# Both heads' exponentials in one instruction over two PSUM banks, in the first four head pairs of an attention and mixer kernel

## The chip, the cores and the metric

One core of one Trainium2 chip. The metric is device time in microseconds (us), from three runs; next to it stands one profiled execution, whose trace gives every number on a single instruction. PE is TensorE's matmuls, PEld its weight loads, DVE is VectorE, ACT ScalarE, POOL GpSimd, SP SyncE.

## The reference

Eight batches, eight heads, 576 tokens, head size 64, 16 extra "beacon" keys and values ahead of the tokens. Attention is causal over the tokens; a low-rank mix along the sequence (rank 32) with a residual follows, then a two-layer MLP (512 to 2048 to 512) with another residual.

```python
k_all = np.concatenate([beacon_k, k], axis=2)          # 592 keys
v_all = np.concatenate([beacon_v, v], axis=2)
scores = scale * np.matmul(q, k_all.transpose(0, 1, 3, 2))
scores = np.where(causal, -1000000000.0, scores)
a = softmax(scores)
x = np.matmul(a, v_all)                                # to (batch, 576, 512)
u = x + (x.transpose(0, 2, 1) @ U @ V).transpose(0, 2, 1)
out = u + np.maximum(u @ w_ch1, 0.0) @ w_ch2
```

## The kernel before, in words

The work goes by pairs of heads: 32 pairs, four to a batch; pairs 0 to 3 are the first batch. For a pair, blocks of transposes on PE (lines 275 and 281) turn q and k, DVE copies them to SBUF as `qT` and `kT` (line 308; the beacons apart, line 313), and `score_units` computes the transposed scores, keys on partitions. The keys of one head fall into four groups of columns (496, 464, 496 and 208 wide, numbered 0 to 3), each in a PSUM bank of its own. One visit takes two groups of both heads: `sc[0]` groups 0 and 1, `sc[1]` groups 2 and 3. The two heads' score matmuls (line 348) stand on two halves of the array and run side by side. ACT then takes the exponential of each group and head, one instruction each (line 354), from its bank into `expt`, a buffer of one head; four such buffers serve two pairs in turn. A head's attn*V (`av_unit`, line 397) is 15 small matmuls into one bank, a reciprocal and a product on DVE (405, 406).

The causal mask is laid in one of two ways. For the pairs in `ON_PE` (0, 1, 4) PE adds a large negative number to the bank before the scores (line 340). For the others DVE takes a minimum with a mask over the exponentials afterwards (`mask_head`, lines 324 and 326).

The order of all engines is written out by hand (`manual_schedule`): an engine runs its instructions in the order in which they are emitted, and the waits between engines are put in by the build from what each instruction reads and writes. PSUM's eight banks are handed out by `pst`, a queue of emptied banks; each result is a tile of its own, in the bank that has been empty longest. `emptying` gives a bank back when its last reader is emitted. `keep_warm` and `idle` (line 250) emit matmuls without use.

After the first batch's four pairs `first_mix` computes the mix in three pieces: `head` (the matmuls `qtp`, line 489), `begin` (413), `rest` (506). Between them stand the first parts (`part`) of the MLP's first layer (`gps`, line 534), whose results ACT (547) and DVE (549) evict with a relu into `gT`. From there on `fill(n)` puts MLP units between the steps of attention: tiles of 512 tokens, 16 units of the first layer, then 16 of the second (`cps`, line 560). The first `fill(3)` of the stage is followed by the transposes of pair 4. The last 128 rows of the last tile go by `c_piece` in three column pieces (256, 128 and 128 wide, `cph`, line 589), each with its addition (594) and its store (596).

Loads are issued by POOL in the order of emission: q, k and v of the first batches, w1 in four pieces and w2 in two (`emit_w2`, line 195).

Of the kernel before, what the change touches and what calls it, by code (L numbers as in the profile page):

```python
# [1 line left out]

# [28 lines left out]
def kernel(  # L31
# [123 lines left out]
    uT = const.tile([P, NCC, B * S], F16, name="uT", tag="uT")  # L155
    rec = const.tile([P, B * H, NT, 1], F32, name="rec", tag="rec")
    NE = 4
    expts = [const.tile([P, EW], F16, name=f"expt{i}", tag=f"expt{i}") for i in range(NE)]
    kTs = [const.tile([P, NH2, NC * P], F16, name=f"kT{i}", tag=f"kT{i}") for i in range(2)]
    vss = [const.tile([P, NC * H * E], F16, name=f"vs{i}", tag=f"vs{i}") for i in range(2)]  # L160

# [26 lines left out]
        fs = ds(FF // 4 * i, FF // 4)  # L188
        nc.gpsimd.dma_start(out=w1[:, :, fs], in_=w1r[:, :, fs])

    def emit_w2():
        w2r = moe_w_ch2.rearrange("(dc p) c -> p dc c", p=P)
        for i in range(2):
            dcs = ds(NDC // 2 * i, NDC // 2)
            nc.gpsimd.dma_start(out=w2[:, dcs, :], in_=w2r[:, dcs, :])

# [118 lines left out]

        return [lambda: one(1, qT, 0), lambda: one(0, kT, Nb)]

    def score_units(c, qT, kT, ex, early=False):  # L320

        def mask_head(i):
            e4 = ex[i][:, 0:EW].rearrange("p (g w) -> p g w", w=SLOT)[:, :, 0:P]
            nc.vector.tensor_tensor(out=e4, in0=e4, in1=bigmask, op=ALU.min)  # L324
            o, n = blk[(4, 4)], nq[4]
            nc.vector.tensor_tensor(
                out=ex[i][0:n, ds(o, n)], in0=ex[i][0:n, ds(o, n)], in1=mask[0:n, 0:n], op=ALU.min
            )

        def visit(gs, idle=0, by_head=True, between=None):  # L330
            turn = [(g, i) for i in range(2) for g in gs] if by_head else [(g, i) for g in gs for i in range(2)]
            ps = {(g, i): pst([P, 512], F32, name=f"sps{i}") for g, i in turn}
            keep_warm(ps[gs[0], 0], idle)
            if early:
                for g in gs:
                    for i in range(2):
                        for ch, qa, w, o in groups[g]:
                            if ch in (g, 4):
                                n = nq[ch]
                                nc.tensor.matmul(  # L340
                                    ps[g, i][:, ds(o, n)], identb, negmask[:, min(ch, 1), 0:n],
                                    start=ch == g, stop=False, skip_group_check=True,
                                )
            for g in gs:
                for ch, qa, w, o in groups[g]:
                    for i in range(2):
                        hp = slice(D * i, D * i + D)
                        nc.tensor.matmul(  # L348
                            ps[g, i][:, ds(o, w)], kT[hp, c, ds(P * ch, P)], qT[hp, c, ds(qa, w)],
                            start=not early, stop=True, skip_group_check=early,  # L350
                        )

            def exps(g, i):
                nc.scalar.activation(  # L354
                    out=ex[i][:, ds(SLOT * g, gw[g])], in_=ps[g, i][:, 0 : gw[g]], func=AF.Exp, scale=scale
                )
# [15 lines left out]

# [145 lines left out]
    def mlp_units(t0, n, dst, flip, turned=True, last=False):  # L518
# [59 lines left out]
                emptying(ps)  # L578
                nc.sync.dma_start(out=dst(i, m), in_=ob[:m, :])

        def c_piece(i, part):

            o, w, d0, d1 = [
                (0, 2 * P, 0, NDC // 2), (0, 2 * P, NDC // 2, NDC), (2 * P, P, 0, NDC), (3 * P, P, 0, NDC)
            ][part]
            if d0 == 0:
                cps["t"] = pst([P, w], F32, name="cph")
            for dc in range(d0, d1):
                nc.tensor.matmul(  # L589
                    cps["t"], gT["t"][:, dc, ts(i, P)], w2[:, dc, ds(o, w)], start=(dc == 0), stop=(dc == NDC - 1)  # L590
                )
            if d1 == NDC:
                ob = outp.tile([P, w], F32, name="oh", tag="ob")
                nc.vector.tensor_tensor(out=ob, in0=cps["t"], in1=gT["u"][:, i, ds(o, w)], op=ALU.add)
                emptying(cps["t"])
                nc.sync.dma_start(out=dst(i, P)[:, ds(o, w)], in_=ob)

        units += [lambda dc=dc: g_unit(dc) for dc in range(NDC)]
        for i in range((n + P - 1) // P):
            c = c_piece if last and i == n // P - 1 else c_unit  # L600
            units += [lambda i=i, part=part, c=c: c(i, part) for part in range(4)]
        return units, g_part

# [105 lines left out]
    def qkT_of(p):  # L709
# [6 lines left out]
                turns[i] = in_pair(prs[p])[i]  # L716
        return qkT_units(turns, qTs[b], kTs[b % 2], c, copies, Ls[0][0][0] if p == 0 else None)

    def expts_of(p):
        return [expts[(2 * p + i) % NE] for i in range(2)]  # L720

    def scores_of(p):
        b, c = divmod(p, NH2)
        return score_units(c, qTs[b], kTs[b % 2], expts_of(p), p in ON_PE)

    def masks_of(p):
        scores_of(p)[2]()
# [1 line left out]
    def av_of(p):  # L729
        b, c = divmod(p, NH2)  # L730
        if c == 0:
            xbs[b] = xbp.tile([P, NT, DM], F16, name="xb", tag="xb")
        return [
            lambda i=i: av_unit(b, 2 * c + i, expts[(2 * p + i) % NE], vss[b % 2], xbs[b]) for i in range(2)
        ]


    NF = 2
    ON_PE = (0, 1, 4)
    AHEAD = 16  # L740

    DT0 = 4
# [50 lines left out]
    with tc.manual_schedule(engines={ENG.PE, ENG.Activation, ENG.DVE, ENG.SP, ENG.Pool}):  # L793
# [58 lines left out]
        mask_head = sc[3]  # L852
# [298 lines left out]
```

## Time and profile before

| | |
|---|---|
| median of three runs | 351.49 us (350.92 to 352.44) |
| the profiled execution's own time | 351.05 us |
| its span, first to last instruction | 349.4 us |
| mean granted TensorE clock | 0.998 |
| PE busy | 342.7 us, 98% |
| ACT busy | 164.2 us, 47% |
| DVE busy | 190.2 us, 54% |

The span is cut by the profile into stretches and groups. A row of the timeline has the start in the span, the time from there to the end of the last instruction merged into it, the engine, the line, the operation, what is written and read, and a count; brackets hold the idle time ahead of it and what ended it. A row of the waits has the total, the count and the longest. A row of a table by stretches has the stretch, then each engine's busy time and count in the order PE, PEld, DVE, ACT, POOL, then the granted clock, the share and the rate of the DMA engines. A row of DMA issues has the queue, the count, the size of one and the median time from issue to landing.

### The profile page before, as it was taken

The numbers are of one execution on the slowest core, as the hardware profiler recorded it, in microseconds if no ns is written. First come the engines' busy times: TensorE is split into PE (matmuls) and PEld (weight loads), VectorE is DVE, ScalarE is ACT, GpSimd is POOL, SyncE is SP. The second block draws the span as 40 slices with busy tenths as digits, with TensorE's granted clock in tenths as the row PEclk, the third lists the DMA queues.
The fourth block names the chain that finished last, engine by engine and source line by source line (L and its number), as shares of the span: only waits on it lengthen the run. The fifth ranks groups of instructions, "written<-read, shape, count | busy, mean of one in ns | idle before, by whom it ended". The sixth has DMA issues, their size and how long they took to land.

```text
span 349.4 us, 7841 instructions
## 1 busy us (share of the span) xinstructions
PE 342.7 (98%) x3105; PEld 174.1 (50%) x3105; DVE 190.2 (54%) x494; ACT 164.2 (47%) x359; POOL 97.9 (28%) x137
## 2 busy tenths in 40 slices
PE   8999999999999999999999999999999999999995
PEld 4565565455554445545454454445445444444444
DVE  5766865588976554645565455535564643323311
ACT  5967851587831666167524843485335103202400
POOL 8976715327415437401840050000000000000000
PEclk9999999999999999999999999999999999999999
DMA  9999999999997999991999899533121323013011
GB/s 167 134 191 174 171 205 171 226 142 142 105 132 136 171 139 125 152 213 29 127 136 157 174 95 134 138 95 68 62 90 32 61 99 90 2 60 105 18 64 65
DMA packets 146780, 41.89 MB, mean 120 GB/s; under 512 B 131504, under 2 KB 142224, under 8 KB 146736
## 3 DMA queue, kind: packets, MB, share of 16 engines
q0 software_dynamic: 87440, 18.18, 66.8%
q1 hardware_dynamic: 59072, 22.84, 37.0%
q8 instruction: 26, 0.43, 0.5%
q10 hardware_dynamic: 224, 0.30, 0.3%
q14 instruction: 18, 0.15, 0.1%
HBM read 37.37 MB, written 9.44 MB: 134 GB/s over the span
## 4 chain that ended last, share of the span: by engine, by line
PE 95%; ACT 2%; DVE 1%; issue 0%
PE gps L534 36%; PE cps L560 35%; PE po L397 8%; PE sps L382 5%; PE sps L348 3%; ACT expt L354 2%; PE tps L275 1%; PE idle L250 1%; PE cph L589 1%; PE qtp L434 1%; PE tps L281 1%; PE ups L459 1%; PE ups L413 1%; DVE qT L308 0%; PE qtp L489 0%; DVE kT L308 0%
## 5 line engine op out<-in xcount | busy, mean ns | idle before, releaser
L534 PE MATMUL gps<-uT,w 128*128 128x512 f16 x576 | 135.7, 379 | 0.1
L560 PE MATMUL cps<-w,gT 128*128 128x512 f16 x560 | 130.6, 379 | 0.0
L388 ACT ACTIVATE expt<-sps 128x496 f16<-128x496 f32 (+2 forms) x152 | 65.3, 537 | 63.9 <-PE sps L382 63.9
L547 ACT ACTIVATE gT<-gps 128x512 f16<-128x512 f32 x86 | 51.8, 619 | 79.8 <-PE gps L534 78.0
L534 PEld LDWEIGHTS <-w 128*128 128x128 f16 x576 | 51.6, 98 | 58.5 <-issue 4.2
L560 PEld LDWEIGHTS <-gT 128*128 128x128 f16 x560 | 51.0, 98 | 57.7 <-issue 3.9
L549 DVE TENSOR_SCALAR gT<-gps 128x512 f16<-128x512 f32 x58 | 40.1, 691 | 43.6 <-PE gps L534 41.9
L354 ACT ACTIVATE expt<-sps 128x496 f16<-128x496 f32 (+1 forms) x104 | 44.7, 589 | 6.7 <-PE sps L348 6.7
L573 DVE TENSOR_TENSOR ob<-cps,ut 128x512 f32<-128x512 f32 x31 | 21.4, 690 | 44.1 <-PE cps L560 43.4
L218 POOL DMA_DIRECT2D vs<-in_v_dram x50 | 39.6, 811 | 15.7 <-DMA w<-in_moe_w_ch_dram 5.9
L397 PEld LDWEIGHTS <-expt 128*128 128x128 f16 (+1 forms) x960 | 36.4, 98 | 14.4 <-issue 2.2
L397 PE MATMUL po<-vs,expt 128*128 128x65 f16 (+1 forms) x960 | 39.4, 194 | 0.1
L406 DVE TENSOR_TENSOR xb<-po,rec 128x320 f16<-128x320 f32 x64 | 31.4, 491 | 2.2
L324 DVE TENSOR_TENSOR expt<-expt,bigmask 128x512 f16<-128x512 f16 x58 | 24.2, 417 | 14.0 <-ACT expt L388 12.4
L405 DVE RECIPROCAL rec<-po 128x5 f32<-128x5 f32 x64 | 12.0, 188 | 22.8 <-PE po L397 22.7
L200 POOL DMA_DIRECT2D vs<-in_beacon_v_dram x8 | 4.3, 536 | 58.1 <-PE po L397 58.1
L382 PE MATMUL sps<-qT,kT 64*128 64x496 f16 (+2 forms) x228 | 18.5, 281 | 0.0
L649 POOL DMA_DIRECT2D st<-in_q_dram x20 | 16.9, 869 | 2.7 <-DMA vs<-in_v_dram 1.4
L649 POOL DMA_DIRECT2D st<-in_k_dram x20 | 16.9, 875 | 1.9 <-DMA vs<-in_v_dram 1.9
L446 DVE TENSOR_TENSOR uT<-ups,uT 128x496 f16<-128x496 f32 x24 | 14.5, 667 | 3.9 <-PE ups L459 3.1
L382 PEld LDWEIGHTS <-kT 64*128 64x128 f16 x228 | 7.9, 94 | 14.6 <-issue 11.9
L348 PE MATMUL sps<-qT,kT 64*128 64x80 f16 (+3 forms) x156 | 14.0, 282 | 0.7 <-DVE qT L308 0.6
(97 smaller groups left out, 169.3 us busy)
## 6 DMA issues: line engine op xcount, KB each, us to landing
out_dram<-ob SPq DMA_DIRECT2D x35, 256.0 KB, 2.5
vs<-in_v_dram POOLq DMA_DIRECT2D x18, 128.0 KB, 7.9
w<-in_moe_w_ch_dram POOLq DMA_DIRECT2D x4, 512.0 KB, 6.1
w<-in_moe_w_ch_dram POOLq DMA_DIRECT2D x2, 1024.0 KB, 13.4
st<-in_k_dram POOLq DMA_DIRECT2D x12, 128.0 KB, 7.4
st<-in_q_dram POOLq DMA_DIRECT2D x12, 128.0 KB, 10.9
st<-in_k_dram POOLq DMA_DIRECT2D x2, 576.0 KB, 12.9
st<-in_q_dram POOLq DMA_DIRECT2D x2, 576.0 KB, 15.7
```

The lines of the kernel that those rows point to most:

```text
L218: nc.gpsimd.dma_start(out=dst[a : a + nq[j], j, :, :], in_=src[hs, ds(q0[j], nq[j]), :].rearrange("h p d -> p h d"))
L348: nc.tensor.matmul(ps[g, i][:, ds(o, w)], kT[hp, c, ds(P * ch, P)], qT[hp, c, ds(qa, w)], start=not early, stop=True, skip_group_check=early,)
L354: nc.scalar.activation(out=ex[i][:, ds(SLOT * g, gw[g])], in_=ps[g, i][:, 0 : gw[g]], func=AF.Exp, scale=scale)
L382: nc.tensor.matmul(ps[p, g, i][:, ds(o, w)], kT[hp, c, ds(P * ch, P)], qT[hp, c, ds(qa, w)], start=True, stop=True,)
L388: nc.scalar.activation(out=at[p][3][i][:, ds(SLOT * g, gw[g])], in_=ps[p, g, i][:, 0 : gw[g]], func=AF.Exp, scale=scale)
L397: nc.tensor.matmul(po[:, j, :], ex[0 : nk[c], ds(blk[(c, j)], P)], vs[0 : nk[c], ds(c * H * E + h * E, E)], start=(c == 0), stop=(c == j),)
L406: nc.vector.tensor_tensor(out=xb[:, :, ds(h * D, D)], in0=po[:, :, 0:D], in1=r.broadcast_to([P, NT, D]), op=ALU.mult)
L534: nc.tensor.matmul(g[:, 0:n], w1[:, cc, ts(dc, P)], uT[:, cc, ds(t0, n)], start=(cc == 0), stop=(cc == NCC - 1))
L547: nc.scalar.activation(out=gT["t"][:, dc, 0:n], in_=g[:, 0:n], func=AF.Relu)
L549: nc.vector.tensor_scalar_max(out=gT["t"][:, dc, 0:n], in0=g[:, 0:n], scalar1=0.0)
L560: nc.tensor.matmul(ps[:m, :], gT["t"][:, dc, ds(P * i, m)], w2[:, dc, :], start=(dc == 0), stop=turned and dc == NDC - 1, skip_group_check ...
L649: nc.gpsimd.dma_start(out=dst[a : m[j], j, :, :], in_=src[:, ds(q0[j], nq[j]), :].rearrange("h p d -> p h d"))
```

## The change

Until pair 3 is done, all eight banks are one tile `banks` of 128 x 8 x 512, and `pst` gives out slices of it. `two` makes a view of two banks of it, with the distance between them as a step, and `exps_of_two` takes the exponential of one group of both heads in one instruction through that view. So the two heads' `expt` buffers become one tile, `expt2`. There are three of these: the third lies in the second half of w2, which is loaded after pair 2 has used it; pairs 0, 1, 2, 3 use buffers 0, 1, 2, 0. The order of a visit is by group, with both heads together. Pair 2 joins `ON_PE`. When all banks are empty after the first `fill(3)`, the one-tile pool is closed and the pool of before is opened. In the last tile the columns go in two halves of 256.

```diff
@@
-    psum = ctx.enter_context(tc.tile_pool(name="ps", bufs=1, space=bass.MemoryType.PSUM))
+    head_psum = ExitStack()
+    banks = head_psum.enter_context(tc.tile_pool(name="hps", bufs=1, space=bass.MemoryType.PSUM)).tile(
+        [P, 8, 512], F32, tag="banks", name="banks"
+    )
+    psum = []
@@ def pst(shape, dtype, name):
         b = emptied.pop(0)
-        t = psum.tile(shape, dtype, tag=f"bank{b}", name=name)
+        if psum:
+            t = psum[0].tile(shape, dtype, tag=f"bank{b}", name=name)
+        else:
+            t = banks[0 : shape[0], b, :]
+            t = (t if dtype == F32 else t.bitcast(dtype))[:, 0 : math.prod(shape[1:])]
+            if len(shape) == 3:
+                t = t.rearrange("p (a b) -> p a b", a=shape[1])
         bank_of[id(t)] = (b, t)
         return t
+
+    def two(t, u, w):
+        a, b = bank_of[id(t)][0], bank_of[id(u)][0]
+        return banks[:, a : b + 1 : b - a, 0:w]
@@ def clear():
-        for i in range(NE):
+        for i in range(len(expts)):
@@
-    expts = [const.tile([P, EW], F16, name=f"expt{i}", tag=f"expt{i}") for i in range(NE)]
+    expt2 = [const.tile([P, 2, EW], F16, name=f"expt{i}", tag=f"expt{i}") for i in range(NE // 2)]
+    spare = w2[:, NDC // 2 :, :].rearrange("p a b -> p (a b)")[:, 0 : 2 * EW]
+    expt2.append(spare.rearrange("p (i e) -> p i e", i=2))
+    expts = [e[:, i, :] for e in expt2 for i in range(2)]
@@
-    def emit_w2():
+    def emit_w2(i):
         w2r = moe_w_ch2.rearrange("(dc p) c -> p dc c", p=P)
-        for i in range(2):
-            dcs = ds(NDC // 2 * i, NDC // 2)
-            nc.gpsimd.dma_start(out=w2[:, dcs, :], in_=w2r[:, dcs, :])
+        dcs = ds(NDC // 2 * i, NDC // 2)
+        nc.gpsimd.dma_start(out=w2[:, dcs, :], in_=w2r[:, dcs, :])
@@ def visit(gs, idle=0, by_head=True, between=None):
             ps = {(g, i): pst([P, 512], F32, name=f"sps{i}") for g, i in turn}
+            for g in gs if not psum else ():
+                if bank_of[id(ps[g, 0])][0] > bank_of[id(ps[g, 1])][0]:
+                    ps[g, 0], ps[g, 1] = ps[g, 1], ps[g, 0]
...
+            def exps_of_two(g):
+                src = two(ps[g, 0], ps[g, 1], gw[g])
+                nc.scalar.activation(out=both[:, :, ds(SLOT * g, gw[g])], in_=src, func=AF.Exp, scale=scale)
+
+            if not psum:
+                for n, g in enumerate(gs):
+                    if between and n:
+                        between()
+                    exps_of_two(g)
+                    emptying(ps[g, 0])
+                    emptying(ps[g, 1])
+                return
+
             for n, (g, i) in enumerate(turn):
@@
-        def c_piece(i, part):
-
-            o, w, d0, d1 = [
-                (0, 2 * P, 0, NDC // 2), (0, 2 * P, NDC // 2, NDC), (2 * P, P, 0, NDC), (3 * P, P, 0, NDC)
-            ][part]
...
+        def c_half(i, part):
+            hs = ds(DM // 2 * (part // 2), DM // 2)
+            if part % 2 == 0:
+                cps["t"] = pst([P, DM // 2], F32, name="cph")
+            for dc in range(NDC // 2 * (part % 2), NDC // 2 * (part % 2 + 1)):
                 nc.tensor.matmul(
-                    cps["t"], gT["t"][:, dc, ts(i, P)], w2[:, dc, ds(o, w)], start=(dc == 0), stop=(dc == NDC - 1)
-                )
...
+                    cps["t"], gT["t"][:, dc, ts(i, P)], w2[:, dc, hs], start=(dc == 0), stop=(dc == NDC - 1)
+                )
+            if part % 2:
...
@@
+    def turn_of(p):
+
+        return {2: 2, 3: 0}.get(p, p % 2)
...
     def expts_of(p):
-        return [expts[(2 * p + i) % NE] for i in range(2)]
+        return [expts[2 * turn_of(p) + i] for i in range(2)]
@@
-    ON_PE = (0, 1, 4)
+    ON_PE = (0, 1, 2, 4)
@@
-        emit_w2()
+        emit_w2(0)
@@ for p in range(2):
-            mask_head = sc[3]
             sc = scores_of(p + 2)
-            if p:
-                mask_head(0)
             sc[0](0, av[1])
-            if p:
-                mask_head(1)
@@
         rest(0, 2, act_copy)
+        emit_w2(1)
         head(2, 1)
@@
         fill(3)
+        assert not bank_of
+        head_psum.close()
+        psum.append(ctx.enter_context(tc.tile_pool(name="ps", bufs=1, space=bass.MemoryType.PSUM)))
         t0, sc = qkT_of(4), scores_of(4)
```

More of the change, by code (lines that the diff above doesn't have):

```diff
@@ L1 @@
+import math
 from contextlib import ExitStack
@@ L318, in qkT_units, with score_units @@
         return [lambda: one(1, qT, 0), lambda: one(0, kT, Nb)]
-    def score_units(c, qT, kT, ex, early=False):
+    def score_units(c, qT, kT, ex, both, early=False):
         def mask_head(i):
@@ L579, in c_unit @@
                 nc.sync.dma_start(out=dst(i, m), in_=ob[:m, :])
-        def c_piece(i, part):
-            o, w, d0, d1 = [
-                (0, 2 * P, 0, NDC // 2), (0, 2 * P, NDC // 2, NDC), (2 * P, P, 0, NDC), (3 * P, P, 0, NDC)
-            ][part]
-            if d0 == 0:
-                cps["t"] = pst([P, w], F32, name="cph")
-            for dc in range(d0, d1):
+        def c_half(i, part):
[3 more added lines that the diff above has]
+            for dc in range(NDC // 2 * (part % 2), NDC // 2 * (part % 2 + 1)):
                 nc.tensor.matmul(
-                    cps["t"], gT["t"][:, dc, ts(i, P)], w2[:, dc, ds(o, w)], start=(dc == 0), stop=(dc == NDC - 1)
+                    cps["t"], gT["t"][:, dc, ts(i, P)], w2[:, dc, hs], start=(dc == 0), stop=(dc == NDC - 1)
                 )
-            if d1 == NDC:
-                ob = outp.tile([P, w], F32, name="oh", tag="ob")
-                nc.vector.tensor_tensor(out=ob, in0=cps["t"], in1=gT["u"][:, i, ds(o, w)], op=ALU.add)
+            if part % 2:
+                ob = outp.tile([P, DM // 2], F32, name="oh", tag="ob")
+                nc.vector.tensor_tensor(out=ob, in0=cps["t"], in1=gT["u"][:, i, hs], op=ALU.add)
                 emptying(cps["t"])
-                nc.sync.dma_start(out=dst(i, P)[:, ds(o, w)], in_=ob)
+                nc.sync.dma_start(out=dst(i, P)[:, hs], in_=ob)
         units += [lambda dc=dc: g_unit(dc) for dc in range(NDC)]
         for i in range((n + P - 1) // P):
-            c = c_piece if last and i == n // P - 1 else c_unit
+            c = c_half if last and i == n // P - 1 else c_unit
             units += [lambda i=i, part=part, c=c: c(i, part) for part in range(4)]
@@ L733, in av_of @@
         return [
-            lambda i=i: av_unit(b, 2 * c + i, expts[(2 * p + i) % NE], vss[b % 2], xbs[b]) for i in range(2)
+            lambda i=i: av_unit(b, 2 * c + i, expts_of(p)[i], vss[b % 2], xbs[b]) for i in range(2)
         ]
     NF = 2
-    ON_PE = (0, 1, 4)
+    ON_PE = (0, 1, 2, 4)
     AHEAD = 16
```

4 lines of the change are left out of this document (3 added, 1 removed).

## The prediction

> **What bounds the kernel now.** I read the page first: busy shares, slices, and the chain that ended last.
>
> ```profile
> PE 342.7 (98%) x3105; PEld 174.1 (50%) x3105; DVE 190.2 (54%) x494; ACT 164.2 (47%) x359; POOL 97.9 (28%) x137
> PE   8999999999999999999999999999999999999995
> PE 95%; ACT 2%; DVE 1%; issue 0%
> ```
>
> TensorE (PE) carries 95% of the chain; ScalarE (ACT) is on it for 2%. The timeline of the first 30 us shows where ACT counts.
>
> ```profile
> 7.28 13.22 ACT L354 ACTIVATE expt<-sps 128x496 f16<-128x496 f32 x32 [0.70 <-PE sps L348]
> 11.19 0.25 PE L340 MATMUL sps<-negmask,identb 128*128 128x128 bf16 x2 [0.23 <-ACT expt L354]
> 21.35 1.06 ACT L686 ACTIVATE uT<-ups 128x496 f16<-128x496 f32 x2 [0.85 <-PE ups L506]
> ```
>
> From 7.28 to 20.50 us ACT runs the 32 exponentials of the first four pairs with no pause, and PE beside it now and then waits for a bank (0.23 us at 11.19). So in this stage ACT sets the pace and PE works around it. Behind it PE is never without work for long; all that its matmuls waited for in the whole span is:
>
> ```profile
> PE idle L250 <- DVE ones L153: 1.2, 1, 1.2
> PE sps L348 <- DVE qT L308: 0.6, 2, 0.3
> PE sps L340 <- ACT expt L354: 0.2, 1, 0.2
> ```
>
> None of that lies after the first stage. Whatever the first 30 us lose or win therefore reaches the end of the span almost whole.
>
> **What one exponential costs, and what pairing saves.** The first one, alone, takes 0.58:
>
> ```profile
> 7.28 0.58 ACT L354 ACTIVATE expt<-sps 128x496 f16<-128x496 f32 x1 [0.70 <-PE sps L348]
> ```
>
> The second of the two 496-column copies at 21.35 adds 1.06 - 0.58 = 0.48. The other 31 exponentials take 13.22 - 0.58 = 12.64 for 13312 - 496 = 12816 columns (a head has 496 + 464 + 208 + 496 = 1664, eight heads). With f fixed and c per column: 496c + f = 0.48 and 12816c + 31f = 12.64 give c = 0.84 ns and f = 0.06 us. Sixteen instructions fewer save 16 x 0.06 = 1.0 us, if ACT stays fed. A paired one takes 0.06 + 0.83 = 0.89 us (992 columns), 0.84 (928) or 0.41 (416) behind another, and 1.00, 0.95 or 0.52 from idle, until others may go on. No row has a two-bank read: if the second bank cost the fixed part again, nothing is saved (+0.06 each, 1.0 in all); I take none. By the Trainium skill, "ScalarE: Activation LUTs", section "What ACT_TABLE_LOAD costs", back-to-back instructions leave 186 - 93 = 93 ns fixed, an estimate of 1.5 us saved; the rows give 1.0.
>
> **What the change adds: waits.** The eight banks become slices of one tile `banks`. In the instruction list of the built program every wait is a count, and matching counts to instructions shows what the diff doesn't: a paired exponential that reads banks a and b is kept apart from every other engine's access to any bank from a to b, the banks between them too, and reads by VectorE (DVE) count. E0 to E15 are the sixteen paired exponentials, four a pair, with their banks; "score" is the matmul pair of two heads, T a block of transposes.
>
> ```
> T of pair 1 (bank 3)                   waits E0  (1,7)
> masks in bank 1                        wait  E1  (0,2)
> E3 (1,7)                               waits DVE copy of qT out of bank 4
> second mask of pair 1 (bank 3)         waits E3  (1,7)
> masks in bank 1                        wait  E4  (0,3)
> T of pair 2 (bank 3), attn*V behind it waits E7  (0,7)
> E8 (1,4)                               waits DVE product out of bank 2
> masks of pair 2 (bank 2)               wait  E8  (1,4)
> scores of pair 3 (bank 2)              wait  E11 (1,4)
> scores of pair 3 (bank 4)              wait  E13 (3,7)
> qtp of the first mix (bank 1)          waits E15 (0,2)
> ```
>
> In each of these the engine's whole queue stands: PE and ACT are in order. The blocks last:
>
> ```profile
> 6.88 0.58 PE L348 MATMUL sps<-qT,kT 64*128 64x496 f16 x4
> 7.39 0.45 PE L281 MATMUL tps<-ident,st 96*64 96x96 f16 x12
> 7.78 0.43 PE L275 MATMUL tps<-ident,pr 96*128 96x96 f16 x6
> 7.88 0.76 DVE L308 COPY kT<-tps 128x576 f16<-128x576 f16 x1 [0.44 <-PE tps L281]
> 8.04 0.57 PE L340 MATMUL sps<-negmask,identb 128*128 128x128 bf16 x6
> 8.55 0.48 PE L348 MATMUL sps<-qT,kT 64*128 64x208 f16 x8
> 8.63 0.75 DVE L308 COPY qT<-tps 128x576 f16<-128x576 f16 x1
> 9.18 0.47 PE L340 MATMUL sps<-negmask,identb 128*128 128x112 bf16 x4
> 9.58 0.58 PE L348 MATMUL sps<-qT,kT 64*128 64x496 f16 x4
> 12.16 0.63 PE L397 MATMUL po<-vs,expt 128*128 128x65 f16 x15
> 12.95 0.18 DVE L405 RECIPROCAL rec<-po 128x5 f32<-128x5 f32 x1
> 13.17 0.49 DVE L406 TENSOR_TENSOR xb<-po,rec 128x320 f16<-128x320 f32 x1
> ```
>
> A waiter starts some 0.05 after its release (T ends at 7.39 + 0.45 = 7.84, the copy starts at 7.88). Between masks and scores lie 0.51 for six masks (8.04 to 8.55) and 0.40 for four (9.18 to 9.58), so 0.055 a mask; both hold waits, and I take 0.06 for the rest of a block freed at once: 0.38 for six, 0.28 for four, 0.23 for three. The first scores of a second visit are done 0.26 after their start, all at 0.48. The chain, in us:
> - E0 waits for the last of four score matmuls, 6.88 + 0.58 = 7.46: it runs 7.50 to 8.50, E1 to 9.33.
> - T of pair 1 starts at 8.55, not 7.39; both T blocks take 0.65. Masks in bank 1 at 9.38, scores at 9.66, E2 from 9.96 to 10.48.
> - The DVE copies follow T: kT at 9.04, qT 0.75 later, to 10.54. E3: 10.58 to 11.58.
> - Second mask of pair 1 at 11.63 (before, among those at 9.18), scores 0.23 later, those that E4 needs done 0.58 on, at 12.44: E4 12.48 to 13.48, E5 to 14.32.
> - Masks 13.53, scores 13.91, the first done at 14.17, before E5 ends: E6 to 14.73, E7 to 15.62.
> - T of pair 2 at 15.67, attn*V of head 0 16.06 to 16.69; DVE copies qT from 16.17 to 16.92, then reciprocal and product (13.17 + 0.49 - 12.95 = 0.71) to 17.5 or so. E8 waits for that: 17.55 to 18.55, E9 to 19.39.
> - Masks of pair 2, now on PE, at 18.60; E10 to 19.80, E11 to 20.69. Scores of pair 3 at 20.74: E12 21.34 to 22.34, E13 to 23.18. Scores in bank 4 at 23.23, E14 23.54 to 24.54, E15 to 24.95.
>
> ACT ends at 24.95 instead of 20.50: 1.0 saved, 5.5 of new idling. And the order behind it bites: the first mix's qtp, which stood in the middle of ACT's stream, now stands behind its end.
>
> ```profile
> 18.75 0.72 PE L489 MATMUL qtp<-xb,Usb 112*32 112x256 f16 x5
> 25.06 1.90 PE L534 MATMUL gps<-uT,w 128*128 128x512 f16 x8
> 26.57 0.69 DVE L549 TENSOR_SCALAR gT<-gps 128x512 f16<-128x512 f32 x1 [1.16 <-PE gps L534]
> 26.78 1.08 ACT L547 ACTIVATE gT<-gps 128x512 f16<-128x512 f32 x2 [1.07 <-PE gps L534]
> 26.89 0.71 PE L281 MATMUL tps<-ident,st 96*64 96x96 f16 x24
> ```
>
> It starts at 25.00, not 18.75: **+6.25**. What follows (attn*V of the third and fourth pair, the mix, the parts of the MLP) keeps its order up to 26.89. There the one-tile pool is closed, and the first transposes of pair 4 wait for its last readers, both relu evictions: 26.78 + 1.08 = 27.86 plus 0.05, against 26.89: **+1.0**. Before, they ran beside those evictions.
>
> The Trainium skill, "PSUM — Partial Sum Buffer", section "PSUM bank collisions raise a hardware error", says that two engines collide in the same bank alone, reads included. By it the banks in between need no wait; the sum goes by the waits that were built, and what would follow from it is the second rival.
>
> **What I cost at nothing.** Pair 2's four DVE masks (each as below, 1.2 us together) leave DVE, off the path in the new order; the ten mask matmuls in their place are in the chain above.
>
> ```profile
> 17.01 0.41 DVE L324 TENSOR_TENSOR expt<-expt,bigmask 128x512 f16<-128x512 f16 x1
> 17.34 0.19 DVE L326 TENSOR_TENSOR expt<-expt,mask 80x80 f16<-80x80 f16 x1
> 36.15 1.07 POOL L195 DMA_DIRECT2D w<-in_moe_w_ch_dram  x1 [0.43 <-issue]
> 52.27 2.76 PE L560 MATMUL cps<-w,gT 128*128 128x512 f16 x12
> ```
>
> w2's second half serves as pair 2's exponentials, so its load (36.15, same place in GpSimd's queue) waits for attn*V of that pair, done in the chain at 25.00 + 0.72 + 0.63 = 26.4; the queue is at 36 anyway, so neither it nor the token loads behind it move. Its first use, in the stretch at 52.27, moves back with PE. Were that cover gone, PE would wait for the landing. Four more memsets on DVE are some 0.2 us, inside E0's wait.
>
> **The tail.** 32 matmuls of 256 columns replace 16 of 256 and 32 of 128: the same columns. The last addition grows, and so does the last transfer.
>
> ```profile
> 343.34 0.42 DVE L594 TENSOR_TENSOR oh<-cph,ut 128x256 f32<-128x256 f32 x1 [1.05 <-PE cph L589]
> 345.12 0.29 DVE L594 TENSOR_TENSOR oh<-cph,ut 128x128 f32<-128x128 f32 x1 [0.60 <-PE cph L589]
> out_dram<-oh SPq DMA_DIRECT2D x1, 128.0 KB, 1.7
> out_dram<-oh SPq DMA_DIRECT2D x2, 64.0 KB, 2.7
> ```
>
> 0.42 - 0.29 = +0.13 for the addition. The transfer of 128 KB landed 1.0 sooner than those of 64 KB, but other transfers were about then, and the closing sequence may hide it: -0.9 to +0.1, I take **+0.1**.
>
> **The sum.** 6.25 + 1.0 + 0.1 = +7.4 on the profiled execution's own 351.05 (span 349.4): 358.5. The median of the runs, 351.49, stands 0.44 above that execution; the range covers it. With the bounds (two-bank cost up to +1.0, tail down to -0.9, a tenth or so at each of eleven waits) this case spans 356.5 to 360.5.
>
> **The rivals.**
> - *Clock* (0.12), slower still. PE now stands idle for 0.4 to 1.5 us at a time between short blocks in the chain above. In this trace eight 512-column matmuls took 3.60 us at the start and 1.90 once warm:
>
> ```profile
> 1.19 3.60 PE L250 MATMUL idle<-w 128*128 128x512 f16 x8 [1.19 <-DVE ones L153]
> 10.00:20.00 10.00, 9.06 (x186) 6.37 (x185) 7.59 (x22) 10.00 (x26) 9.37 (x16) 1.00 1.38 151
> ```
>
>   Should PE fall back to that half speed between 10 and 31 us, some 8 us of PE work in the chain grows by about 5, and the first dense matmuls behind it by 1.7: some +6 more, 364.5. Against it: the row of 10 to 20 us shows a granted clock of 1.00 with PE gaps already there. "TensorE: Matmul & The Clock Gate" of the Trainium skill, section "A second HAM failure mode: psum-queue depth-cycling", says that just such micro-idling lets the clock oscillate; this trace shows no oscillation.
> - *Covered waits* (0.05), faster. The place is the second mask of pair 1: if E3 were over before PE comes to it (9.2), and likewise at the other waits, the new waits would cost nothing, ACT would save its 1.0, and the tail its 0.9: 349.2. It decides whether PE reaches a bank before the exponential spanning it ends; the row at 11.19 shows PE already there first, so little speaks for it.
> - *Absorbed* (0.05). The stage ends late, but PE makes it up where it used to wait: about 352. PE's waits above sum to 2.0 us, 1.2 of them before the stage; it can't hold 7.
>
> **How the numbers follow.** Forecast 0.78. A measurement can tell this kernel from no change by about 0.5%, 1.8 us. Faster 0.05, within 0.05, slower 0.78 + 0.12 = 0.90. The range leaves out both small rivals (0.10) and the worse half of the clock case: 355.0 to 364.5.
>
> **What would show it.** Right: sixteen exponentials with idle gaps, E15 ending near 25; qtp near 25; pair 4's transposes near 34 behind relu evictions; then the same stretches, some 7.4 later. Wrong: exponentials back to back ending near 19.5; transposes starting beside the evictions; or the first 30 us as computed and later stretches catching up; or granted clock below 1 between 10 and 31.

## The result, and the profile after

The changed kernel takes 362.11 us (median of six runs, 361.18 to 363.62), the kernel before on the same chip 351.57 (350.92 to 352.44): the ratio is 1.0302, 95% interval 1.0274 to 1.033. It is slower, as forecast, but by 10.5 us where the sum of the forecast was 7.4. The mean granted clock is 0.978 to 0.988 in every one of the six runs, against 0.998 in the profiled execution of before. The profiled execution took 363.62, its span is 362.0, 12.6 more than before's.

The page after, the same three lines as before and the line of the granted clock:

```profile
PE 348.2 (96%) x3099; PEld 178.0 (49%) x3099; DVE 189.3 (52%) x493; ACT 163.8 (45%) x343; POOL 98.0 (27%) x137
PE   7689899999999999999999999999999999999995
PEclk9867999999999999999999999999999999999998
PE 93%; ACT 2%; DVE 1%; DMA 1%; issue 1%; ACTq 0%; DVEq 0%
```

All that is new lies in the first four of the 40 slices (9 us each): PE, which was at 8 and 9 tenths there, is at 7, 6, 8, and the clock, which stood at full speed in before's stage, is at 8, 6 and 7 tenths. PE has 5.5 us more busy time with fewer instructions: the same work at a lower clock.

The timeline of ScalarE from 7 us (start, duration, operation, count, idle before it and what ended it):

```profile
7.34 1.83 ACT L380 ACTIVATE expt<-banks 128x992 f16<-128x992 f32 x2 [0.85 <-PE banks L368]
9.80 0.52 ACT L380 ACTIVATE expt<-banks 128x416 f16<-128x416 f32 x1 [0.63 <-PE banks L368]
10.54 1.00 ACT L380 ACTIVATE expt<-banks 128x992 f16<-128x992 f32 x1 [0.22 <-DVE qT L325]
12.45 3.15 ACT L380 ACTIVATE expt<-banks 128x992 f16<-128x992 f32 x4 [0.92 <-PE banks L368]
18.25 1.83 ACT L380 ACTIVATE w<-banks 128x992 f16<-128x992 f32 x2 [2.65 <-PE banks L368]
21.17 1.41 ACT L380 ACTIVATE w<-banks 128x416 f16<-128x416 f32 x2 [1.09 <-PE banks L368]
23.70 1.83 ACT L380 ACTIVATE expt<-banks 128x992 f16<-128x992 f32 x2 [1.12 <-PE banks L368]
26.27 1.41 ACT L380 ACTIVATE expt<-banks 128x992 f16<-128x992 f32 x2 [0.75 <-PE banks L368]
```

And PE's, three rows behind it:

```profile
27.73 1.22 PE L522 MATMUL banks<-xb,Usb 112*32 112x256 f16 x5 [0.44 <-ACT expt L380]
...
36.03 1.90 PE L567 MATMUL banks<-uT,w 128*128 128x512 f16 x8
38.89 0.71 PE L298 MATMUL tps<-ident,st 96*64 96x96 f16 x24 [0.96 <-ACT gT L580]
```

Where before had one row of 32 exponentials without a pause, there are now eight rows with idle time ahead of each: 7.4 us between the first and the last. The sixteenth ends at 26.27 + 1.41 = 27.68; the first mix's qtp follows at 27.73, and pair 4's transposes start at 38.89, behind the relu evictions.

What PE's matmuls waited for, in us, times, and the longest:

```profile
PE banks L298 <- ACT expt L380: 2.4, 2, 1.3
PE banks L360 <- ACT expt L380: 1.9, 2, 1.2
PE banks L368 <- ACT expt L380: 1.4, 1, 1.4
PE tps L298 <- ACT gT L580: 1.0, 1, 1.0
PE banks L522 <- ACT expt L380: 0.4, 1, 0.4
```

Transposes, masks, scores and qtp now wait for exponentials, 6.1 us in all. Before's whole list had 0.2 of that kind.

The windows of 5 us (the first number behind the window is its length, the next PE's busy time; the three at the end are the granted clock, the share of DMA, GB/s):

```profile
5.00:10.00 5.00, 3.69 (x55) 2.35 (x54) 2.93 (x9) 3.46 (x7) 5.00 (x8) 1.00 1.33 141
10.00:15.00 5.00, 2.43 (x35) 1.49 (x35) 1.86 (x18) 3.87 (x6) 5.00 (x8) 1.00 1.41 133
15.00:20.00 5.00, 4.35 (x62) 3.13 (x61) 1.84 (x5) 2.35 (x3) 3.68 (x9) 0.52 1.32 145
20.00:25.00 5.00, 3.86 (x64) 2.67 (x61) 3.07 (x8) 2.79 (x5) 4.25 (x7) 0.80 1.27 192
25.00:30.00 5.00, 3.98 (x47) 2.97 (x47) 1.61 (x6) 1.93 (x3) 1.88 (x4) 0.54 1.43 196
30.00:35.00 5.00, 5.00 (x63) 3.50 (x62) 2.70 (x9) 1.69 (x4) 4.46 (x7) 0.77 1.53 158
```

From 10 to 15 us PE is busy for 2.43 of 5. Behind that the clock falls to 0.52, comes back, and falls again to 0.54. So two cases of the prediction came together: the waits that it forecast, and the fall of the clock that it held for a rival.

### The profile page after: what moved, and what is told of

It reads as the page before. It is cut to its first block, busy times and chain, and to the rows that moved or that the text cites. A ratio compares the mean times of both kernels' runs of the same rounds, so it can differ in the third digit from the quotient of the medians.

```text
span 362.0 us, 7804 instructions
## 1 busy us (share of the span) xinstructions
PE 348.2 (96%) x3099; PEld 178.0 (49%) x3099; DVE 189.3 (52%) x493; ACT 163.8 (45%) x343; POOL 98.0 (27%) x137
## 4 chain that ended last, share of the span: by engine, by line
PE 93%; ACT 2%; DVE 1%; DMA 1%; issue 1%; ACTq 0%; DVEq 0%
PE gps L567 34%; PE cps L593 34%; PE po L430 7%; PE sps L415 5%; PE sps L368 2%; ACT expt L380 2%; PE banks L430 1%; PE banks L368 1%; PE tps L292 1%; DMA stk<-in_k_dram 1%; PE cph L619 1%; PE qtp L467 1%; PE banks L298 1%; PE banks L567 1%; PE ups L492 1%
## 5 line engine op out<-in xcount | busy, mean ns | idle before, releaser
L567 PE MATMUL gps<-uT,w 128*128 128x512 f16 x564 | 132.6, 379 | 0.1
L580 ACT ACTIVATE gT<-gps 128x512 f16<-128x512 f32 x84 | 50.6, 618 | 80.4 <-PE gps L567 77.7
L235 POOL DMA_DIRECT2D vs<-in_v_dram x50 | 39.8, 811 | 13.5 <-PE tps L298 4.8
L430 PEld LDWEIGHTS <-expt 128*128 128x128 f16 x930 | 36.3, 99 | 14.4 <-issue 2.4
L430 PE MATMUL po<-vs,expt 128*128 128x65 f16 (+1 forms) x840 | 34.4, 194 | 0.0
L374 ACT ACTIVATE expt<-sps 128x496 f16<-128x496 f32 x72 | 31.4, 550 | 6.0 <-PE sps L368 6.0
L341 DVE TENSOR_TENSOR expt<-expt,bigmask 128x512 f16<-128x512 f16 x56 | 23.4, 418 | 14.0 <-ACT expt L421 12.4
L439 DVE TENSOR_TENSOR xb<-po,rec 128x320 f16<-128x320 f32 x56 | 27.5, 492 | 1.9
L438 DVE RECIPROCAL rec<-po 128x5 f32<-128x5 f32 x56 | 10.5, 188 | 21.7 <-PE po L430 21.6
L217 POOL DMA_DIRECT2D st<-in_beacon_k_dram x8 | 4.5, 561 | 36.0 <-DVE pr L287 21.0
## 6 DMA issues: line engine op xcount, KB each, us to landing
w<-in_moe_w_ch_dram POOLq DMA_DIRECT2D x2, 1024.0 KB, 12.8
```

Source lines behind the costliest of these rows:

```text
L235: nc.gpsimd.dma_start(out=dst[a : a + nq[j], j, :, :], in_=src[hs, ds(q0[j], nq[j]), :].rearrange("h p d -> p h d"))
L374: nc.scalar.activation(out=ex[i][:, ds(SLOT * g, gw[g])], in_=ps[g, i][:, 0 : gw[g]], func=AF.Exp, scale=scale)
L430: nc.tensor.matmul(po[:, j, :], ex[0 : nk[c], ds(blk[(c, j)], P)], vs[0 : nk[c], ds(c * H * E + h * E, E)], start=(c == 0), stop=(c == j),)
L439: nc.vector.tensor_tensor(out=xb[:, :, ds(h * D, D)], in0=po[:, :, 0:D], in1=r.broadcast_to([P, NT, D]), op=ALU.mult)
L567: nc.tensor.matmul(g[:, 0:n], w1[:, cc, ts(dc, P)], uT[:, cc, ds(t0, n)], start=(cc == 0), stop=(cc == NCC - 1))
L580: nc.scalar.activation(out=gT["t"][:, dc, 0:n], in_=g[:, 0:n], func=AF.Relu)
```

## The experiments

All are compared with before's runs on the same chip (351.40 to 351.44). Line numbers in the rows are each kernel's own.

**Neighbouring banks, first try.** The score blocks of one exponential take a couple of banks, (0,1), (2,3) or (4,5), in `take_couple`; single blocks prefer banks 6 and 7:

```diff
-        b = emptied.pop(0)
+        b = couple.pop(0) if couple else emptied.pop(next((n for n, e in enumerate(emptied) if psum or e > 5), 0))
...
+                take_couple()
...
```

> The changed kernel, but the two score blocks that one exponential reads always lie in neighbouring banks (0,1), (2,3) or (4,5), so that the stretch from the first to the second holds no bank of anybody else; order, exponentials, masks, pool change and tail stay. Theory (waits on the banks in between): exponentials come nearly back to back again, the sixteenth ends near 19.5 to 20.5 us in place of 27.7, the granted clock stays 1.00 between 10 and 35 us, and of the 10.5 us lost only the pool change (+1.0) and the tail (+0.1) are left, against some 1.0 saved on ScalarE: 351 to 352.5. Rival one (a read over two banks, or the new order of pair 2's masks, costs by itself, whichever banks): 357 to 362, with the gaps between the exponentials still there. Rival two (the clock falls for a reason of its own, not for PE's gaps): the exponentials are back to back but PE's granted clock is still below 1 between 15 and 35 us, 355 to 357.

Measured: 359.42 (357.21 to 360.46), ratio 1.0224 (1.0198 to 1.025). Neither the theory's 351 to 352.5 nor, by the trace, the first rival: the exponentials are nearly back to back, from 9.04 to 20.08 + 3.13 = 23.21, 14.17 us in place of the changed kernel's 20.34. What was lost is this kernel's own doing. Some of PE's waits,

```profile
PE banks L274 <- ACT qT L726: 1.6, 1, 1.6
PE banks L456 <- DVE xb L449: 1.5, 2, 0.9
```

and ScalarE's timeline, the first and the last row of exponentials:

```profile
9.04 1.83 ACT L390 ACTIVATE expt<-banks 128x992 f16<-128x992 f32 x2 [0.67 <-PE banks L378]
...
20.08 3.13 ACT L390 ACTIVATE expt<-banks 128x992 f16<-128x992 f32 x4 [0.49 <-PE banks L378]
```

With two banks for all single blocks, the first transposes waited 1.6 us for a copy, and the mix after the stage queued up for the same two. The clock fell here too, to 0.91 from 5 to 10 us and 0.75 from 10 to 15, behind that first wait. Its time decides nothing; it is mended below.

**Single exponentials.** Pairing alone undone:

```diff
-                    exps_of_two(g)
+                    for i in range(2):
+                        exps(g, i)
```

> The changed kernel, but each head's exponential is an instruction of its own over one bank, as before; the one tile of eight banks, the pool change, pair 2's masks on TensorE and the tail stay. Theory (waits come from the read over a stretch of banks, and from nothing else in the change): 32 exponentials without gaps that end near 20.5 us, clock 1.00, and only the pool change (+1.0) and tail (+0.1) are left: 352 to 353. Rival (the one tile by itself, or the masks, bring the waits): 357 to 362.

Measured: 352.88 (352.26 to 353.18), ratio 1.0038 (1.0025 to 1.0051), clock 1.00 in each window of the stage. The theory's 352 to 353. The one tile of eight banks, the masks on TensorE and the pool change bring hardly any of the waits of the stage (PE waits 0.4 us in all for exponentials, in place of 6.1); all but some 1.4 us of the loss comes with the read over two banks. The last row of exponentials in ScalarE's timeline,

```profile
17.87 3.38 ACT L374 ACTIVATE expt<-banks 128x496 f16<-128x496 f32 x8 [0.30 <-PE banks L368]
```

and in PE's waits:

```profile
PE tps L298 <- ACT gT L581: 1.0, 1, 1.0
```

The exponentials end at 21.25 with 0.64 of pauses (the 0.30 shown and one of 0.34), not quite the gapless 20.5 expected; pair 4's transposes wait the 1.0 of the pool change.

**One pool.** The tile of eight banks is never closed, and later blocks are slices of it too:

```diff
...
-        head_psum.close()
-        psum.append(ctx.enter_context(tc.tile_pool(name="ps", bufs=1, space=bass.MemoryType.PSUM)))
+        psum.append(None)
```

> The changed kernel, but the tile of eight banks is never closed: all later PSUM tiles are slices of it too, so that pair 4's transposes wait for their own bank alone. Theory: they start about 1.0 us sooner, beside the relu evictions, nothing else of the first 36 us changes, and the time falls by 1.0 to about 361 (360 to 362). Rival (the barrier only takes up time that PE would lose later): no change, 362. Rival (a tile of eight banks held to the end brings waits of its own in the later pairs, whose exponentials read one bank each): longer than 362.

Measured: 361.33 (361.21 to 361.86), ratio 1.0282 (1.0269 to 1.0295): 0.8 less than the changed kernel. In PE's timeline, the eight matmuls ahead of pair 4's transposes, and those transposes:

```profile
35.61 1.90 PE L563 MATMUL banks<-uT,w 128*128 128x512 f16 x8
...
37.44 0.71 PE L294 MATMUL banks<-ident,st 96*64 96x96 f16 x24
```

They start 1.83 behind the first of the eight, where the changed kernel needed 38.89 - 36.03 = 2.86: 1.03 gone, with no idle time ahead of them. The clock fell in another place here (0.64 already from 10 to 15 us), so the time alone would carry less; the pair of kernels at the end gives the same 1.0 without that.

**The tail alone,** in the kernel before:

```diff
-            o, w, d0, d1 = [
-                (0, 2 * P, 0, NDC // 2), (0, 2 * P, NDC // 2, NDC), (2 * P, P, 0, NDC), (3 * P, P, 0, NDC)
-            ][part]
+            hs = ds(DM // 2 * (part // 2), DM // 2)
...
```

> The kernel before with the change's tail alone: the last row block's second half as one piece of 256 columns. Prediction: +0.1 from the longer last addition (bounds -0.9 to +0.1): 351.6, and the stretch from the last addition's end to the span's end as long as before (4.0 us). Rival (the one larger transfer lands sooner than the last of two small ones and the end follows it): 350.6 to 351.0, that stretch near 3.0.

Measured: 350.98 (350.67 to 352.43), ratio 0.9991 (0.9979 to 1.0002), which can't be told from no change; the median alone lies where the rival put it (350.6 to 351.0). The last addition in VectorE's timeline,

```profile
345.33 0.42 DVE L591 TENSOR_TENSOR oh<-cph,ut 128x256 f32<-128x256 f32 x1 [1.32 <-PE cph L586]
```

and the last transfers, with the us from issue to landing:

```profile
out_dram<-oh SPq DMA_DIRECT2D x2, 128.0 KB, 2.5
```

From the addition's end (345.75) to the span's end (349.3) are 3.55; before, 345.41 to 349.4, 3.99. The one profile lies between the two expectations (4.0 and 3.0).

**Filling one gap.** Six matmuls of 512 columns in place of one while PE waits for E3:

```diff
-    IDLE = [8, 1, 1, 0, 1]
+    IDLE = [8, 1, 6, 0, 1]
```

> The changed kernel with six matmuls of 512 columns in place of one ahead of pair 1's first masks: they write bank 0, whose contents the next matmul replaces, and fill the 1.24 us (10.35 to 11.59) in which TensorE stands idle for E3; no wait is taken away, and E3 ends where it did (11.54). Theory (TensorE loses its clock to that idle time): the granted clock stays 1.00 through 15 to 20 us, or falls later and for a shorter time, E15 ends near 25 in place of 27.7, and the time falls by 2 to 4.5 us to 357.5 to 360 (358.5 if no phase of half clock is left). Rival one (the clock falls for another reason, or any of the later gaps of 0.7 to 1.3 us is enough for it): 361 to 363, granted clock near 0.5 between 15 and 20 us as in the changed kernel. Rival two (the filling delays the masks and with them the chain): over 363.

Measured: 361.89 (359.86 to 363.22), ratio 1.0278 (1.0249 to 1.0308). The time is that of rival one; the trace shows what the theory called a later fall. Windows,

```profile
5.00:10.00 5.00, 2.69 (x41) 1.86 (x41) 2.32 (x5) 3.26 (x6) 5.00 (x9) 1.00 1.39 136
...
15.00:20.00 5.00, 3.43 (x76) 2.65 (x75) 2.52 (x6) 2.92 (x4) 3.17 (x8) 1.00 1.23 142
20.00:25.00 5.00, 3.27 (x73) 2.48 (x70) 2.29 (x7) 3.76 (x6) 3.92 (x6) 0.96 1.21 185
25.00:30.00 5.00, 4.37 (x52) 3.58 (x50) 2.73 (x10) 0.90 (x2) 2.47 (x4) 0.50 1.41 197
30.00:35.00 5.00, 5.00 (x39) 2.78 (x38) 1.59 (x5) 1.81 (x5) 3.94 (x7) 0.52 1.68 166
```

and, in PE's timeline, the row ahead of the fall:

```profile
24.00 0.48 PE L368 MATMUL banks<-qT,kT 64*128 64x336 f16 x8 [1.39 <-ACT expt L380]
```

The clock is full where the changed kernel had 0.52, and falls some nine microseconds later, behind a gap of 1.39 (up to 24.00), to stay at half up to 34 (the window from 30 to 35). A gap of 1.28 up to 16.24 had passed without a fall. The filling moved the slow phase; it didn't remove it.

**Filling four gaps,** run after this. The filling just shown stays, and `hold(n, b)` puts n more matmuls into bank b in three other places: ahead of pair 1's second masks, of pair 3's second scores and of the first qtp:

```diff
...
+            if p == 0:
+                hold(3, 6)
...
+        hold(6, 0)
...
+        hold(4, 3)
```

> The last filling experiment filled one gap; its clock then held until 24.4 us and fell behind the next gaps (1.39 us of idle up to 24.00, 0.63 up to 25.95). This kernel fills those too: besides the six matmuls ahead of pair 1's first masks, three in bank 6 ahead of its second masks (they wait for E4), six in bank 0 ahead of pair 3's second scores (they wait for E13) and four in bank 3 ahead of the first qtp (it waits for E15). No wait is taken away; all the banks hold nothing that is still read. Theory (the lost time is two things, the waits' +7.4 and a clock that PE's idle gaps bring down): granted clock 1.00 from 5 to 40 us, E15 ends 17.5 to 18.0 us after E0 starts, pair 4's transposes near 34.5, and 358.0 to 359.5 us, that is 2.5 to 4 less than the changed kernel. Rival one (the clock falls whatever TensorE does in the gaps, or in the one gap of 1.3 us that can't be filled): still 361 to 363. Rival two (fillers delay the chain by up to their own length): clock 1.00 but 360 to 362.

Measured: 358.51 (358.33 to 359.00), ratio 1.0202 (1.0188 to 1.0216). This is the value of the theory. Its windows,

```profile
10.00:15.00 5.00, 4.81 (x55) 2.60 (x53) 2.42 (x20) 3.46 (x5) 4.91 (x7) 1.00 1.44 133
15.00:20.00 5.00, 3.42 (x75) 2.64 (x76) 2.51 (x6) 2.92 (x4) 3.82 (x8) 1.00 1.29 149
20.00:25.00 5.00, 4.56 (x82) 2.92 (x79) 2.29 (x7) 3.76 (x6) 3.61 (x7) 1.00 1.27 185
25.00:30.00 5.00, 4.96 (x81) 3.57 (x78) 3.55 (x13) 2.16 (x5) 2.67 (x4) 1.00 1.43 197
```

the first and the last exponentials,

```profile
7.95 1.83 ACT L384 ACTIVATE expt<-banks 128x992 f16<-128x992 f32 x2 [0.93 <-PE banks L372]
...
24.50 1.41 ACT L384 ACTIVATE expt<-banks 128x992 f16<-128x992 f32 x2 [0.54 <-PE banks L372]
```

and the PE rows that the changed kernel had at 27.73, 36.03 and 38.89:

```profile
25.95 0.71 PE L526 MATMUL banks<-xb,Usb 112*32 112x256 f16 x5
...
32.26 1.90 PE L571 MATMUL banks<-uT,w 128*128 128x512 f16 x8
35.11 0.71 PE L302 MATMUL tps<-ident,st 96*64 96x96 f16 x24 [0.96 <-ACT gT L584]
```

PE still waits for the same exponentials, only with matmuls in place of idle time, and work that nobody needs was added; the kernel is 3.6 us faster than the changed one. Its five runs have a mean clock of 0.999 or 1.000, the changed kernel's six 0.978 to 0.988. With the clock at 1.00 the exponentials take 25.91 - 7.95 = 17.96 us from the first start to the last end (20.34 before the filling), and the qtp block 0.71 in place of 1.22. So the loss of the change is two things: 358.51 - 351.44 = 7.1 of waits with their sequel, and 362.11 - 358.51 = 3.6 of clock (the runs of the two, 361.18 to 363.62 and 358.33 to 359.00, don't overlap).

**Pair 2's masks on TensorE alone,** in the kernel before:

```diff
-    ON_PE = (0, 1, 4)
+    ON_PE = (0, 1, 2, 4)
...
-            if p:
-                mask_head(0)
...
-            if p:
-                mask_head(1)
```

> The kernel before with pair 2's masks on TensorE alone: ten mask matmuls more (0.55 us of TensorE) ahead of its scores, four VectorE masks fewer (1.2 us). Theory: ScalarE sets the pace of this stage, so that the ten matmuls lie beside its exponentials and cost nothing: 351.2 to 351.8, exponentials without a pause until 20.5. Rival (the stage is as much TensorE's): pauses between exponentials appear at pair 2's scores, and up to 0.55 more: 352.0.

Measured: 351.55 (351.14 to 352.32), ratio 1.0000 (0.9988 to 1.0012). The time is the theory's, but the pauses that the rival forecast are there, in ScalarE's timeline:

```profile
16.05 1.53 ACT L354 ACTIVATE expt<-sps 128x208 f16<-128x208 f32 x4 [0.42 <-PE sps L348]
17.83 3.38 ACT L354 ACTIVATE expt<-sps 128x496 f16<-128x496 f32 x8 [0.24 <-PE sps L348]
```

**Neighbouring banks, mended,** with the pool change, and then with one pool:

```diff
...
+        low = 4 if not taken else 6 if len(taken) < 16 else 0
+        b = couple.pop(0) if couple else emptied.pop(next((n for n, e in enumerate(emptied) if e >= low), 0))
...
```

> The first experiment again (the two score blocks of an exponential in neighbouring banks (0,1), (2,3) or (4,5)), with its own fault mended: there the transposes ahead of the first exponential had only banks 6 and 7 and started 1.6 us late, and after pair 3 the blocks still queued up for these two. Now the first transposes go round four banks, and after pair 3's scores all eight are used in turn again. Theory (the waits come from the banks in between): first exponential near 7.3, sixteenth's end at 20 to 21.5, granted clock 1.00 from 5 to 35 us, pool change +1.0, tail -0.3: 351.5 to 353. Rival (two-bank reads or the new order of masks cost by themselves): gaps of 0.5 us and more between exponentials, over 355.

> Neighbouring banks as in the kernel just named, and the tile of eight banks never closed: both added waits taken away. Theory: 1.0 less than with the pool change, 350.5 to 352, level with the kernel before or up to 1 us below it. Rival (three couples of banks in turn are too few: TensorE waits for the couple that the exponential three places back still reads): gaps of 0.3 to 0.5 us between exponentials eat the 1.0 saved, 351.5 to 353, slower than before by 0 to 1.5.

Measured: 352.99 (352.69 to 353.55), ratio 1.0040 (1.0028 to 1.0051), and 351.98 (351.72 to 352.55), ratio 1.0012 (1.0001 to 1.0023). The exponentials in ScalarE's timeline of the first:

```profile
7.32 6.16 ACT L392 ACTIVATE expt<-banks 128x992 f16<-128x992 f32 x8 [0.81 <-PE banks L380]
13.79 3.16 ACT L392 ACTIVATE w<-banks 128x992 f16<-128x992 f32 x4 [0.32 <-PE banks L380]
17.43 3.13 ACT L392 ACTIVATE expt<-banks 128x992 f16<-128x992 f32 x4 [0.48 <-PE banks L380]
```

and the rows about pair 4's transposes in PE's timeline of the second:

```profile
26.00 1.90 PE L575 MATMUL banks<-uT,w 128*128 128x512 f16 x8
27.83 0.71 PE L303 MATMUL banks<-ident,st 96*64 96x96 f16 x24
```

The same sixteen paired reads, in couples with no bank between them, end at 20.56 in place of 27.68: that settles the cause of the waits. Without the pool change the transposes again start 1.83 behind the eight matmuls, and the time falls by 352.99 - 351.98 = 1.0. But even so the kernel is not below the one before: pauses of 0.32 and 0.48 ahead of pairs 2 and 3 eat what the pairing saves (the rival of the second).

**Masks and scores group by group,** to take these pauses away:

```diff
...
             for g in gs:
+                if early and not psum:
+                    mask_of(g)
...
```

> Neighbouring banks and one pool as in the last but one, and the two score blocks of a group get masks and scores together, group after group, in place of the masks of both groups first: TensorE then waits for the couple that the exponential three places back has read, not two. Theory (the gaps of 0.32 and 0.48 us between exponentials come from that order): they go, the sixteenth ends near 19.7 in place of 20.8, and the time falls by 0.3 to 0.8: 351.2 to 351.7. Rival (the gaps come from the transposes and attn*V that TensorE does ahead of those scores, so that TensorE itself sets the pace there): no change, 351.8 to 352.2.

Measured: 352.41 (nine of ten runs 352.16 to 353.25, one 355.62), ratio 1.0030 (1.0020 to 1.0040). That is nearer to the rival than to the theory, and a little slower than either. The last exponentials in ScalarE's timeline,

```profile
16.90 3.50 ACT L393 ACTIVATE w<-banks 128x992 f16<-128x992 f32 x4 [0.61 <-PE banks L381]
21.08 3.13 ACT L393 ACTIVATE expt<-banks 128x992 f16<-128x992 f32 x4 [0.68 <-PE banks L381]
```

show that the pauses ahead of pairs 2 and 3 did not go: they are 0.61 and 0.68, at a clock of 1.00 from 15 us on. The profiled execution is the one of 355.62, and earlier in it the clock had fallen, to 0.75 from 5 to 10 us and 0.57 from 10 to 15, so its first exponentials tell nothing about the order; the other nine runs have a mean clock of 0.997 to 1.000. What brings the two pauses stays open. No version beat the kernel before by more than can be measured.

## Why the prediction was right, and where it fell short

**Right, step by step.** *Cost of an exponential*: a paired one of 992 and one of 928 columns from idle took 1.83 (forecast 1.00 + 0.83), the 416 alone 0.52 (0.52), four behind one another 3.15 (3.14); the second bank costs nothing that these rows show. The two equations as printed give f = 0.046 and c = 0.875 ns, not 0.06 and 0.84: they hang on the 0.48, which is rounded to 0.01, and a hundredth there moves f by 0.05. So the forecast's 1.0 was less certain than it looked. The mended couples bear it out, as they give the saving itself: 6.16 + 3.16 + 3.13 = 12.45 busy against 13.22, with two more starts from idle at 0.11 each, so 1.0 saved. The estimate of 1.5 from the Trainium skill ("ScalarE: Activation LUTs", "What ACT_TABLE_LOAD costs") is not borne out here.

*The chain*: E3's end 11.54 (forecast 11.58), E4's start 12.45 (12.48), E7's end 15.60 (15.62), though E0 began 0.16 sooner than forecast, so that the chain itself took some 0.1 longer. All waits up to there are where the instruction list put them. With the clock held the rest follows too, 17.96 against 17.45 from E0's start to E15's end. Part of the 0.5 is a slip: at E8 the prediction's own figures give 16.92 + 0.71 = 17.63 for the product, not 17.5. *The order behind it*: qtp starts 0.05 after E15 in the changed kernel and 0.04 in the one with four fillings, as forecast; with the clock held, qtp to pair 4's transposes is 35.11 - 25.95 = 9.16, forecast 34.14 - 25.00 = 9.14. *The pool change*: 1.0 forecast, 1.03 and 1.0 measured. The sum, +7.4, is measured as +7.1 in medians. That they come so close is in part luck: from E0's start to pair 4's transposes the kernel with four fillings needs 35.11 - 7.95 = 27.16 where before needs 26.89 - 7.28 = 19.61, so 7.55 in place of the 7.25 summed, and the tail gave 0.5 back.

**Mis-sized, inside its bounds.** *The tail*: +0.1 taken, -0.5 measured (350.98 - 351.44), not to be told from nothing; the lower bound was -0.9. *Pair 2's masks* at nothing: the time is unmoved, but the cover was thinner than told. In before PE was busy for 9.06 of the 10 us from 10 to 20 (the row in the prediction), idle for 0.94, so that nothing that ScalarE does there can bring more than that, and ten more matmuls use up half a microsecond of it (ten times the prediction's 0.055). That "ACT sets the pace and PE works around it" was too strong: they are 0.94 apart.

**Wrong: the clock.** The step that failed is the weighing of the rival *Clock*, which got 0.12 and was kept out of the sum. The argument against it was the row of 10 to 20 us with PE gaps and a clock of 1.00. But in that row PE is busy for 9.06 of 10; in the forecast's own chain it is not, and the prediction never added up the new gaps. The gaps there, 10.1 to 11.6, 12.8 to 13.5 and 14.4 to 15.7, are 3.5 of the 5.6 us from 10.1 to 15.7, and the trace after shows 2.43 busy of 5. The rival's mechanism came true at its place (15 to 35 us, the first departure from the computed chain is E8, 18.25 in place of 17.55), at 3.6 in medians where +6 was priced: the slow phase covered two stretches, not all from 10 to 31. In the profiled execution, which is the longest of the six runs, it took more: from E0's start to pair 4's transposes are 38.89 - 7.34 = 31.55, against 27.16 with the clock held, so 4.4. A granted clock below 1 between 10 and 31 us was among the prediction's own signs of being wrong. The waits alone were allowed 356.5 to 360.5, and 362.11 lies above that; that the whole range holds it is due to the half of this rival's case that the range took in.

The Trainium skill bears on this from two sides. "TensorE: Matmul & The Clock Gate", section "A second HAM failure mode: psum-queue depth-cycling", says that micro-idling between groups of matmuls makes the clock oscillate; the windows after agree (1.00, 0.52, 0.80, 0.54, 0.77, 1.00). The rule of thumb in its section "Why this matters for your kernels", no idle gaps above some 3 us, would have let this kernel pass: its longest wait for an exponential is 1.4 us, and the clock halved. The measurement decides.

**Open.** What exactly the clock goes by. 2.43 busy of 5 us was followed by a fall, 3.27 with a gap of 1.39 in it too, 3.42 with a gap of 1.28 was not; but the kernel with one filling was busy for 2.69 of 5 from 5 to 10 us and kept its clock. And in the profiled execution of the last kernel, masks and scores group by group, PE was busy for 2.12 of the 3 us from 4 to 7, with no gap above 0.6 there, and the clock fell to 0.50 behind it, while the kernel with one filling was busy for 1.69 of the 4 us from 5 to 9 and kept 1.00. No threshold follows from these, neither for the longest gap nor for the busy share. Whether the waits on the banks in between could simply be left out on the chip was not tried, as it would have left reads and writes unordered.

## What to carry to other kernels

The build orders a read over several banks of one tile against every bank from the first to the last, so which banks the pieces get decides what it costs: lay the pieces side by side, or the instruction saved is paid back many times in waits. Before costing a saving on the engine that sets a stage's pace, take the idle time of the next engine in that stage; as long as that engine's work stays the same, it is the most that can be won (0.94 us here; no version with paired reads won any of it). And when an edit makes TensorE wait, add up its busy time per stretch of a few microseconds and give the clock a price of its own: here, half idle, it cost 3.6 us on top of the waits' 7.1. The busy share is a warning and not a rule, as the runs above contradict one another on it.

## What the runs showed of the hardware

- Idle gaps of at most 1.3 us, together half of 5 us (2.43 busy), were followed by a fall of the granted clock from 1.00 to 0.52; with the gaps filled it stayed at 1.00. Once down it stayed down through mostly busy work (in the kernel with one filling from about 25 to 34).
- Eighteen more matmuls whose results nobody reads, put into four gaps, won 3.6 us (362.11 to 358.51) without taking away a wait; filling one gap of several (five more) only moved the slow phase.
- A ScalarE read over two banks costs per column what one over a single bank costs, with one fixed part of 0.06 us (four paired reads behind one another took 3.15, forecast 3.14).
